# A wait ahead of each input load of batches 2 to 7: four loads under way in a fused attention and token-mixing kernel

## The chip, the cores and the metric

The kernel runs on one core of a Trainium2 chip. The time is in microseconds (us) on the device, from runs of the whole program. Beside it stands one profiled execution, with a trace of every instruction and every DMA packet. Its span runs from the first to the last instruction of the program; the time of the execution contains a little more.

The engines have these names: PE (TensorE, matmuls and transposes; PEld is its loading of weights), DVE (VectorE), ACT (ScalarE), POOL (GpSimd) and SP (SyncE, which only issues DMAs here). L91 is line 91 of the kernel.

## What is computed

Inputs are q, k and v of shape 8 x 8 x 576 x 64 (batch, head, position, head dimension) in float32, and three weight matrices. Attention is done within chunks of 64 positions; its output, seen as 8 x 576 x 512, goes through a layer that mixes positions:

```python
# attention in chunks of 64 positions
scores = scale * np.matmul(q_c, k_c.transpose(0, 1, 2, 4, 3))
scores = scores - np.max(scores, axis=-1, keepdims=True)
attn = np.exp(scores)
attn = attn / (np.sum(attn, axis=-1, keepdims=True) + 1e-09)
out = np.matmul(attn, v_c)
...
# mixing of positions, x of shape 8 x 576 x 512
wq = x @ w_q
wk = x @ w_k
W_tok = scale * np.einsum('bsd,btd->bst', wq, wk)
mixed = np.einsum('bst,btd->bsd', W_tok, x)
return (np.maximum(mixed, 0.0) @ w_out).astype(np.float32)
```

## The kernel before

**Units and batches.** The attention of all 8 batches is cut into 36 units of 8 chunk pairs; a batch is 4.5 units (9 tiles, two to a unit). A unit passes through these stages: `stage_a1` (L365) transposes tiles of q and k on TensorE (L375), `stage_a2` copies them to SBUF on DVE (L385), `stage_b1` makes the scores (L400) and their maxima on DVE (L408), `stage_b2` subtracts them (L414) and takes the exponential on ACT (L422), `stage_c` transposes the result (L429) and copies it (L431), `stage_d1` multiplies with v (L445), `stage_d2` divides by the sums (L457 to L460) and leaves the output in `x_nat`. The loop from L525 overlaps the stages: in step kk it does b1 of unit kk, d1 of unit kk-2, a1 of unit kk+2, c of unit kk-1.

**The mixing layer.** The steps of a batch's mixing layer (`make_moe`, L151) are set into this loop by a plan that is made when the program is built (L472 on). Each engine takes its instructions in the order in which the program lists them; nothing is reordered at run time. The layer's outputs (L320, L338) are copied to `osb` and stored by DMAs on SP's queue (L321, L340).

**The input loads.** All loads are DMAs issued by GpSimd, one after the other; they read float32 and write float16. `load_qk(b, part)` (L85) issues four: q and k, each in two halves of the partitions' heads (`sl`), for tiles 0 to 3 (part 0) or 4 to 8 (part 1). Each writes 128 KB or 160 KB. `load_v(b, part)` (L94) sets the column of ones with a memset (L98) and issues three: one over 128 partitions and two over 64, 128 + 64 + 64 KB or 160 + 80 + 80 KB. A batch has 14 loads. There are two buffers for each kind and part of tile, so the loads of batch b + 2 write where those of batch b were read.

**When they are issued.** The loads of batches 0 and 1 are listed at the start (L119 to L125), v's second part of batch 1 a little later. `reload` (L506) lists a load of batch b + 2 right after the last stage that reads the same part of batch b: `load_qk` after `stage_a1`, `load_v` after `stage_d1`. The weights are loaded behind `load_qk(2, 0)` (four loads, L110 and L111) and behind `load_qk(2, 1)` (two, L115). In the whole program GpSimd issues 118 loads: 64 of q and k, 48 of v, 6 of weights. Apart from memsets and the identity matrix it does nothing else.

**What a load waits for.** The framework gives the loads of GpSimd eight completion semaphores in turn, so a load also waits until the load eight places before it has landed. A load into a used buffer waits for TensorE to have read it.

Of the kernel before, what the change touches and what calls it, by code (L numbers as in the profile page):

```python
# [9 lines left out]
F16 = mybir.dt.float16  # L10
# [7 lines left out]
def kernel(  # L18
# [15 lines left out]
    nc = tc.nc  # L34
    B, H, S, D = q.shape
# [3 lines left out]
    P = 128  # L39
# [12 lines left out]
    const = ctx.enter_context(tc.tile_pool(name="const", bufs=1))  # L52
# [28 lines left out]
    cuts = ((0, 4), (4, NT))  # L81
    v_cuts = ((0, 8), (8, NS))
    data = {}

    def load_qk(b, part):  # L85
        t0, t1 = cuts[part]
        for ti, x in enumerate((q, k)):
            tl = qn_pool.tile([P, 2, t1 - t0, R * D], F16, name=f"qn{ti}{part}", tag=f"qn{ti}{part}")
            of = x[b].rearrange("h s d -> (h s) d").rearrange("(l t p r) d -> l p t (r d)", l=2, p=P, r=R)
            for sl in range(2):  # L90
                nc.gpsimd.dma_start(tl[:, sl], of[sl, :, t0:t1, :])  # L91
            data[b, part, ti] = tl

    def load_v(b, part):  # L94
        n0, n1 = v_cuts[part]
        vt = v_pool.tile([P, 2, n1 - n0, D + 2], F16, name=f"vt{part}", tag=f"vt{part}")
        of = v[b].rearrange("h s d -> (h s) d").rearrange("(l n p) d -> l p n d", l=2, p=P)
        nc.gpsimd.memset(vt[:, :, :, D : D + 1], 1.0)  # L98

        for sl, to, at, rows in ((0, 0, 0, P), (1, 0, CH, CH), (1, CH, 0, CH)):  # L100
            nc.gpsimd.dma_start(vt[to : to + rows, sl, :, 0:D], of[sl, at : at + rows, n0:n1, :])  # L101
        data[b, part, 2] = vt

    def w_rows(w):
# [12 lines left out]


    load_qk(0, 0)  # L119
    load_qk(0, 1)  # L120
    load_v(0, 0)
    load_qk(1, 0)
    load_v(0, 1)
    load_qk(1, 1)
    load_v(1, 0)  # L125

    drain = [False]
# [495 lines left out]
```

## Time and profile before

| | us |
|---|---|
| median of 3 runs | 152.61 (152.55 to 152.71) |
| profiled execution, time | 152.53 |
| its span | 150.7 |
| PE busy | 122.2 (81%) |
| DVE busy | 113.9 (76%) |
| ACT busy | 100.9 (67%) |
| POOL busy | 94.3 (63%) |

The DMA issues by kind (from issue to landing is the median of the group):

| from, to | queue | number, KB each | us from issue to landing |
|---|---|---|---|
| q to `qn` | POOL | 16 of 160, 16 of 128 | 5.5, 6.2 |
| k to `qn` | POOL | 16 of 160, 16 of 128 | 5.9, 5.9 |
| v to `vt` | POOL | 8 of 160, 8 of 128 | 6.9, 7.6 |
| v to `vt` | POOL | 16 of 80, 16 of 64 | 5.9, 6.8 |
| weights to `wout` | POOL | 2 of 256 | 6.6 |
| `osb` to the output | SP | 31 of 256, 9 of 128 | 4.1, 3.0 |
| `wqkT` to `wqd` | SP | 6 of 72 | 5.5 |

How to read the lines that follow below. In the view of slices the span is cut into 40 equal parts of some 3.8 us, and each digit is the busy share of one of them in tenths. In the chain of waits and in the timeline the first number is the start in us from the beginning of the span, the second the duration; `x8` is a run of eight instructions; a bracket holds the idle time of the engine before it and what ended it. The chain follows the work that ended last backwards: at each step to what released it. "issue" in it is time for which the profile shows no cause. A line of the DMA issues names the tile, the queue, the number, the size and the time to landing; asked of a short stretch of time, it tells of a single load. A load's bar on POOL is the time in which GpSimd makes its descriptors; the data move afterwards.

### The profile page before, as it was taken

Reading aid. Unit: us, or ns where it says so; the run is one execution under the profiler, and the core shown is the slowest. Engines: PE = TensorE matmul, PEld = TensorE weight load, DVE = VectorE, ACT = ScalarE, POOL = GpSimd, SP = SyncE. Lnnn points to the kernel's source line nnn. Section 1 sums busy time; section 2 is a strip of 40 time slices with the busy share of each in tenths; the row PEclk is TensorE's granted clock in tenths of the full one; section 3 lists DMA queues with packets and bytes.
Section 4 is the critical chain, followed back from the end, with each engine's and each line's share of the span. In section 5 each row is a group of like instructions: output and inputs, shape, how many; then the busy total and the mean of one; then the engine's idle time right before and its main releaser. Section 6 shows DMA issues by size and latency. Waiting matters only on the chain.

```text
span 150.7 us, 6041 instructions
## 1 busy us (share of the span) xinstructions
PE 122.2 (81%) x2580; PEld 83.0 (55%) x2580; DVE 113.9 (76%) x235; ACT 100.9 (67%) x199; POOL 94.3 (63%) x140
## 2 busy tenths in 40 slices
PE   0267767768686999998979999999879988999970
PEld 0156646556464775684747657766657655554430
DVE  0047997999989889998798899989968897454530
ACT  3004334556658979996888899979986996777130
POOL 8999999999789999968878996986000000000000
PEclk9999995999999999999999999999999999999998
DMA  1999999999999999999999999999922344334484
GB/s 17 147 156 163 163 162 165 113 145 145 168 181 166 167 172 192 199 211 212 255 203 217 173 205 220 229 189 244 214 54 74 73 154 157 112 139 106 177 255 165
DMA packets 83050, 25.08 MB, mean 166 GB/s; under 512 B 77392, under 2 KB 78544, under 8 KB 83024
## 3 DMA queue, kind: packets, MB, share of 16 engines
q0 software_dynamic: 77152, 14.82, 118.1%
q1 hardware_dynamic: 5728, 9.75, 19.1%
q8 instruction: 20, 0.33, 0.9%
q10 hardware_dynamic: 144, 0.13, 0.3%
q14 instruction: 6, 0.05, 0.1%
HBM read 29.62 MB, written 9.44 MB: 259 GB/s over the span
## 4 chain that ended last, share of the span: by engine, by line
PE 40%; DVE 16%; ACT 13%; POOL 12%; DMA 11%; issue 5%; DVEq 0%; ACTq 0%; POOLq 0%
PE op L313 11%; POOL qn L91 8%; DMA qn<-in_k_dram 8%; PE tp L375 5%; DVE x_nat L460 4%; DVE sh L414 4%; PE ep L429 4%; DMA out_dram<-osb 3%; ACT es L422 3%; DVE mx L408 3%; POOL vt L101 3%; ACT osb L141 3%; PE tx L165 3%; DVE qkt L385 3%; PE sp L400 3%
## 5 line engine op out<-in xcount | busy, mean ns | idle before, releaser
L101 POOL DMA_DIRECT2D vt<-in_v_dram x48 | 37.9, 824 | 5.6 <-DMA vt<-in_v_dram 3.1
L431 ACT COPY et<-ep 128x512 f16<-128x512 f16 x36 | 21.4, 595 | 18.5 <-PE ep L429 17.2
L375 PE MATMUL tp<-ident,qn 128*64 128x128 f16 x576 | 26.8, 235 | 8.5 <-DMA qn<-in_q_dram 6.1
L385 DVE COPY qkt<-tp 128x1024 f16<-128x1024 f16 x36 | 24.5, 682 | 9.2 <-PE tp L375 9.1
L313 PE MATMUL op<-wout,rmx 128*128 128x512 f16 x124 | 30.5, 379 | 0.2 <-ACT rmx L147 0.2
L422 ACT ACTIVATE es<-sh 128x512 f16<-128x512 f32 x36 | 23.3, 646 | 10.1 <-DVE sh L414 10.1
L408 DVE TENSOR_REDUCE mx<-sp 128x8 f32<-128x512 f32 x36 | 24.7, 686 | 6.8 <-PE sp L400 6.7
L91 POOL DMA_DIRECT2D qn<-in_k_dram x32 | 26.5, 862 | 3.0 <-PE ep L429 1.1
L375 PEld LDWEIGHTS <-qn 128*64 128x64 f16 x576 | 20.4, 118 | 13.1 <-DMA qn<-in_q_dram 6.5
L414 DVE TENSOR_TENSOR sh<-sp,mx 128x512 f32<-128x512 f32 x36 | 24.9, 692 | 3.5
L91 POOL DMA_DIRECT2D qn<-in_q_dram x32 | 27.1, 881 | 0.5 <-issue 0.4
L460 DVE TENSOR_TENSOR x_nat<-xp,rec 128x512 f16<-128x512 f32 x36 | 24.9, 692 | 1.2
L141 ACT COPY osb<-op 128x512 f32<-128x512 f32 (+1 forms) x29 | 17.1, 598 | 7.1 <-PE op L313 5.6
L400 PEld LDWEIGHTS <-qkt 64*64 64x64 f16 x576 | 12.6, 113 | 15.8 <-issue 5.3
L400 PE MATMUL sp<-qkt 64*64 64x64 f16 x576 | 16.8, 200 | 5.0 <-DVE sh L414 2.1
L445 PE MATMUL xp<-vt,et 64*64 64x65 f16 x576 | 13.2, 198 | 7.3 <-DVE x_nat L460 3.6
L141 ACT COPY xt<-tx 128x768 f16<-128x768 f16 (+1 forms) x23 | 18.2, 792 | 0.9 <-PE tx L165 0.9
L313 PEld LDWEIGHTS <-rmx 128*128 128x128 f16 x124 | 11.2, 98 | 10.2 <-issue 0.6
L147 ACT ACTIVATE rmx<-ma 128x512 f16<-128x512 f32 x28 | 15.4, 610 | 1.1 <-PE ma L251 1.0
L429 PE MATMUL ep<-ident,es 128*128 128x128 f16 x144 | 14.7, 226 | 0.0
L445 PEld LDWEIGHTS <-et 64*64 64x64 f16 x576 | 9.4, 108 | 9.2 <-ACT es L422 5.1
L165 PE MATMUL tx<-ident,x_nat 128*128 128x128 f16 x144 | 12.3, 223 | 0.0
(47 smaller groups left out, 139.9 us busy)
## 6 DMA issues: line engine op xcount, KB each, us to landing
out_dram<-osb SPq DMA_DIRECT2D x31, 256.0 KB, 4.1
qn<-in_q_dram POOLq DMA_DIRECT2D x16, 160.0 KB, 5.5
qn<-in_k_dram POOLq DMA_DIRECT2D x16, 160.0 KB, 5.9
qn<-in_q_dram POOLq DMA_DIRECT2D x16, 128.0 KB, 6.2
qn<-in_k_dram POOLq DMA_DIRECT2D x16, 128.0 KB, 5.9
vt<-in_v_dram POOLq DMA_DIRECT2D x8, 160.0 KB, 6.9
vt<-in_v_dram POOLq DMA_DIRECT2D x16, 80.0 KB, 5.9
out_dram<-osb SPq DMA_DIRECT2D x9, 128.0 KB, 3.0
```

Source lines behind the costliest of these rows:

```text
L91: nc.gpsimd.dma_start(tl[:, sl], of[sl, :, t0:t1, :])
L101: nc.gpsimd.dma_start(vt[to : to + rows, sl, :, 0:D], of[sl, at : at + rows, n0:n1, :])
L141: (nc.vector.tensor_copy if on_vector else nc.scalar.copy)(to, of)
L313: nc.tensor.matmul(op[:], lhsT=rmx[:, i, ds(t * P, P)], rhs=wout16[:, i, :], start=(i == 0), stop=(i == HQ - 1),)
L375: nc.tensor.transpose(tp[CH * sl : CH * sl + CH, j, ti, :, r, :], src[:, sl, r * D : r * D + D], ident[:],)
L385: nc.vector.tensor_copy(qkt[:].rearrange("p j t c k -> p (j t c k)"), tp[:].rearrange("p j t c r g -> p (j t c r g)"),)
L400: nc.tensor.matmul(sp[rows, i ^ sl, :], lhsT=qkt[rows, j, 0, c, :], rhs=qkt[rows, j, 1, c, :], start=True, stop=True,)
L408: nc.vector.tensor_reduce(mx[:], sp[:], axis=AX.X, op=ALU.max)
L414: nc.vector.tensor_tensor(out=sh[:].rearrange("p i (g r) -> p i r g", g=G, r=R), in0=sp[:].rearrange("p i (r g) -> p i r g", g=G, r=R), in ...
L422: nc.scalar.activation(es[:], sh[:], AF.Exp, scale=scale_attn)
L445: nc.tensor.matmul(xv[CH * par : CH * par + CH, sl, m, :], lhsT=et[at : at + CH, m, CH * sl : CH * sl + CH], rhs=vt[at : at + CH, sl, 0 : ...
L460: nc.vector.tensor_tensor(out=x_nat[:, 4 * u : 4 * u + 4, :, :].rearrange("p m l d -> p l m d"), in0=xv[:, :, :, 0:D], in1=rec[:, :, :, No ...
```

## The change

Ahead of each load of batches 2 to 7, GpSimd copies one element of the fourth last load of q, k or v into a scratch tile, `probe`, and then issues the load. The copy reads what that load wrote, so it waits for the landing; GpSimd takes its instructions in order, so the load after it waits too. The list `sent` holds one element of each load of q, k and v, in the order of issue; the loads of weights are not in it and have no copy ahead of them. The loads of batches 0 and 1 enter the list but are not held back.

```diff
+    probe = const.tile([P, 1], F16, name="probe")
+    sent = []
+
+    def send(to, of, paced):
+
+        if paced:
+            last = sent[-4]
+            at = last.start_partition()
+            nc.gpsimd.tensor_copy(probe[at : at + 1], last)
+        nc.gpsimd.dma_start(to, of)
 
     def load_qk(b, part):
...
             for sl in range(2):
-                nc.gpsimd.dma_start(tl[:, sl], of[sl, :, t0:t1, :])
+                send(tl[:, sl], of[sl, :, t0:t1, :], b >= 2)
+                sent.append(tl[0:1, sl, 0, 0:1])
             data[b, part, ti] = tl
 
     def load_v(b, part):
...
         for sl, to, at, rows in ((0, 0, 0, P), (1, 0, CH, CH), (1, CH, 0, CH)):
-            nc.gpsimd.dma_start(vt[to : to + rows, sl, :, 0:D], of[sl, at : at + rows, n0:n1, :])
+            send(vt[to : to + rows, sl, :, 0:D], of[sl, at : at + rows, n0:n1, :], b >= 2)
+            sent.append(vt[to : to + 1, sl, 0, 0:1])
         data[b, part, 2] = vt
```

In the changed kernel the copy is line 92 and the issue line 93.

## The prediction

> **What bounds the kernel now.** I read the engine rows and the slices first, then the chain of waits, then GpSimd's timeline, then the time to landing of single loads.
>
> The chain of waits names GpSimd and the loads only in the first third of the span:
>
> ```profile
> 15.71 2.38 POOL qn L91 x3
> 18.09 5.44 DMA qn<-in_k_dram
> 23.57 0.42 PE tp L375 x2
> ...
> 38.14 0.74 POOL qn L91
> 38.88 0.34 issue
> 39.23 6.26 DMA qn<-in_k_dram
> 45.53 0.30 PE tp L375 x3
> ```
>
> A K load issued at 39.23 lands 6.26 us later, and the transposes L375 start 0.04 after it. Up to here the input sets the pace. Later the chain runs through PE, DVE and ACT, and no input load stands in it. But the loads have not become idle work:
>
> ```profile
> POOL 8999999999789999968878996986000000000000
> DMA  1999999999999999999999999999922344334484
> ```
>
> GpSimd and the DMA engines are busy to slice 28 of 40, about 105 us. So the question for the whole change is how much earlier than needed a load lands. I count the loads of GpSimd from 0 to 117 (64 of q and k, 48 of v, 6 of weights). Load 48 is the one of the chain: it lands at 45.49, when it is wanted. Load 111, the last of k, is issued at 97.83; the issue view of that moment has
>
> ```profile
> qn<-in_k_dram POOLq DMA_DIRECT2D x1, 160.0 KB, 8.3
> ```
>
> so it lands at 106.1. Its first reader is the second quarter of this group of TensorE's timeline, some 0.3 us after its start, at 109.85:
>
> ```profile
> 109.54 0.64 PE L375 MATMUL tp<-ident,qn 128*64 128x128 f16 x16
> ```
>
> The slack there is 3.7 us. Between these two loads the DMA engines supply 63 loads in 60.65 us, 0.963 us each, and the computation wants 63 in 64.3 us, 1.02 us each. The margin is 6%. Anything that makes the mean load cost more than about 1.02 us becomes the kernel's pace.
>
> How many loads are under way? GpSimd already has a limit of eight:
>
> ```profile
> 72.13 0.91 POOL L101 DMA_DIRECT2D vt<-in_v_dram  x1
> 73.72 1.38 POOL L101 DMA_DIRECT2D vt<-in_v_dram  x2 [0.68 <-DMA vt<-in_v_dram]
> ```
>
> The load at 73.72 waits for the load eight before it, issued at 65.51 with 7.92 us to landing, so landed at 73.43: the engine starts 0.29 us after the landing. From load 45 on, six or seven earlier loads are in flight at each issue (starts and landings laid side by side).
>
> **The change, part by part.** It removes nothing and reorders nothing; in the instruction order of the changed kernel GpSimd alone gains 84 copies of one element, one ahead of each load of batches 2 to 7 (14 a batch: 8 of q and k, 6 of v). The weights' six loads and batch 1's last three stay free. Each copy waits for the landing of the fourth last load of q, k or v, and behind it in GpSimd's queue stands everything else of GpSimd: this load, the next memset, every later load. Nothing of SP's queue is behind it. Who waits for those loads is TensorE's L375 and L445.
>
> The first part is the copy's own time. The trace has no such copy. GpSimd's nearest rows are 98 ns for a memset of 128x1 and 287 ns for a select over 128x128; below, the DMA after a v memset starts only 0.05 us after the memset's start (7.91 and 7.96), so it may cost as little as 0.05. I take 0.15, nearer to the memset, keeping 0.05 and 0.29. GpSimd's own work per batch is four issues 0.75 apart, four 0.86 apart and six of v for 4.7, together 11.1 us, plus 0.2 for memsets; fourteen copies at 0.15 make it 13.4, or 0.96 us a load. That alone is still under 1.02. At 0.29 it is 15.4, or 1.10, above it.
>
> The second part is the loop that the wait closes: landing of load n-4, 0.29 us to the start of the copy (if it wakes as the DMA did; 0.04 as TensorE's does is the low end), the copy, then issue to landing with three loads ahead. Four loads pass per turn. Its largest term is the last, and it's not the 5.5 to 7.9 us of the page's medians, which is queueing behind seven. Single issues show what is left with a short queue:
>
> ```profile
> qn<-in_q_dram POOLq DMA_DIRECT2D x1, 128.0 KB, 3.2
> ...
> qn<-in_k_dram POOLq DMA_DIRECT2D x1, 128.0 KB, 4.2
> ...
> qn<-in_q_dram POOLq DMA_DIRECT2D x1, 160.0 KB, 4.3
> ```
>
> These are loads 0, 3 and 4, with none, three and four ahead. Load 4 starts at 4.53 and lands at 8.88; load 0, its fourth last, lands at 4.68, so the cap would issue it at 4.68 + 0.29 + 0.15 = 5.12. Loads land in the order of issue and it would still find a queue, so I leave its landing: 3.76 us. The other row in just the capped state is load 36: issued at 29.28, three ahead, the fourth last landed 0.30 before:
>
> ```profile
> qn<-in_q_dram POOLq DMA_DIRECT2D x1, 160.0 KB, 4.3
> ```
>
> 4.25 us. I take the middle of 3.76 and 4.25, 4.0; the bounds are 3.24 (a lone load) and 4.72 (load 5, four ahead and one of the larger loads). A turn is 4.0 + 0.29 + 0.15 = 4.44 us, 1.11 us a load, above the 1.02 wanted and the 0.96 supplied.
>
> The sum. The first copy stands ahead of load 25 and waits for load 21, which lands at 23.53: load 25 goes out at 23.97 instead of 21.21 and lands at 28.0. In the order that the copies count, load 111 is 80 places later, 20 turns: 88.8 us, 116.8. The free loads use GpSimd too (four of wqk 2.7 us, two of wout 1.3 us), and four turns of four issues leave little room; against it three loads of v go out unpaced. I add 2 us net, with 0 and 4 as bounds. Load 111 then lands at 118.8, 9.0 us after 109.85. The same sum puts load 48 (17 places, 18.9 us, plus 2) at 48.9, 3.4 us late, so the delay begins early and grows. What follows load 111 (40.85 us to the end of the span) keeps its length: the drain has no loads but load 112 to 117, six places or 6.7 us after it, wanted 6.3 and 12.5 us after it, so at most 0.4 us more. Nothing hides the 9 us: TensorE waits in order, and DVE, ACT and the stores are fed by it.
>
> The profiled execution took 152.53 us with a span of 150.7; the median of the runs is 152.61. 152.53 + 9.0 gives 161.5.
>
> One rule of the Trainium skill bears on the loop. The page "DMA: Bandwidth & Descriptors", section "Anatomy of one DMA — SWDGE (gpsimd) path", gives a transfer issued by GpSimd a fixed 2.0 us, mostly the wait for the receipt, plus its bytes over 436 GB/s. For 128 KB that would be an estimated 2.3 us against the 3.2 us of load 0, and a turn of some 2.7 us, under which the cap would cost nothing. The row is the measurement and I go by it; the rule's other side, that a round trip is paid per turn and not per byte, is what a cap of four exposes.
>
> **The rivals.**
> First, the harder cap: the loop is longer than I take, because the stores (256 KB each, from 55 us on) slow the loads in flight, or because the copy costs like the select. For it: after 60 us the DMA engines move 205 to 220 GB/s where they moved 144 at first, and time to landing rises at the same seven ahead from 5.3 to 8.3. Against: most of that rise is queue. With 4.25 + 0.29 + 0.29 = 4.83 a turn, load 111 lands at 28.4 + 96.6 + 2 = 127, 17 us late: 169.7. With 4.72 in place of 4.25 it is 26.5 us, 179.
>
> Second, on the other side: four in flight still keep the DMA engines full, and a shorter queue helps what shares them. The point is a turn of 3.85 us (four times 0.963). It needs issue to landing of 3.4 us at my other terms, just over the lone load's 3.24, or 3.76 with the low ends 0.04 and 0.05. Then the loads keep their pace, the late slack of 3.7 us hides the rest, and the gain would be at the transfers of wqd (72 KB, median 5.5 us), for which TensorE's L251 waits 2.2 us in three places. At most that is won: 150.3; with the delay of the first turns given back against it, 152 to 155. Against it: it needs all low ends together, and GpSimd's 0.96 us a load is beside it.
>
> Third, the cap doesn't bite: this would need the waits to be met already, at the place of issue. They are not: for 92 of the 93 loads from 25 on, the fourth last of all loads lands after the issue (by 1.5 to 5 us from load 45 on). A time of 152.6 would come of it.
>
> **How the numbers follow.** My forecast, 3 to 14 us slower, has 0.62. The harder cap has 0.19, the full engines 0.17 (of it 0.06 faster, 0.02 within 0.2%, 0.09 slower by up to 3 us), no bite 0.02. A difference under 0.2% can't be told from none here. Range: 155 (turn of 4.1 and nothing for the free loads: 28 + 82 = 110, plus the early delay of 2.5 us that stays) to 171 (the harder cap's first sum and a little). Faster 0.06, same 0.04, slower 0.90.
>
> **What would show it.** In the changed profile GpSimd's L92 copies should show the idle time, some 15 to 25 us of it, ended by landings of qn and vt; a copy should take about 0.1 to 0.2 us; time to landing on the page should fall from 5.5 to 7.9 to about 4; GpSimd's row should stay filled to about 115 to 120 us instead of 104; TensorE's L375 should wait for qn in batches 3 to 7, by some 9 us together more than now. DVE and ACT should keep their busy times. I am wrong if the loads land every 0.96 us or faster (the second rival), if the copies take more than 0.3 us, or if TensorE waits and the end does not move, which would mean that the tail had room.

## The result, and the profile after

| | before | changed |
|---|---|---|
| median, us | 152.66 (152.55 to 152.75, 4 runs) | 180.3 (180.23 to 182.66, 4 runs) |
| profiled execution, span, us | 150.7 | 178.5 |
| DVE, ACT busy, us | 113.9, 100.9 | 114.9, 101.9 |
| POOL busy, us | 94.3 | 107.2 |

The ratio of the times is 1.185, with a 95% interval of 1.175 to 1.195: 27.6 us slower. That is outside the range, 155 to 171. Some executions of a kernel take over 1.5% longer than its fastest one; the ratios leave them out, the medians hold them.

First the slices and the shares of the chain of waits of the changed kernel, from its profile page:

```profile
POOL 8999849896288878569658888575874300000000
PEclk9999669969955799996999589999996699999997
DMA  4999999999999999999999999999999914413475
...
DMA 37%; POOL 26%; PE 21%; issue 10%; ACT 2%; DVE 2%; POOLq 0%; ACTq 0%; DVEq 0%
```

GpSimd is occupied to slice 32, 143 us instead of 105, but with holes, and the loads with GpSimd's work for them hold 63% of the chain to the end. The same line of the kernel before:

```profile
PE 40%; DVE 16%; ACT 13%; POOL 12%; DMA 11%; issue 5%; DVEq 0%; ACTq 0%; POOLq 0%
```

There the loads and GpSimd held some 20%, for 3 of the 11% of DMA are stores.

The groups of GpSimd's copies (line, engine, operation, tiles and shape, count, then busy time, mean ns of one, idle time before them and what ended it), and TensorE's list of waits (the tile, what it waited for, us in total, times, the longest), changed and then before:

```profile
L92 POOL COPY probe<-qn 1x1 f16<-1x1 f16 x46 | 8.1, 176 | 12.5 <-DMA qn<-in_k_dram 7.6 <-DMA qn<-in_q_dram 4.2
L92 POOL COPY probe<-vt 1x1 f16<-1x1 f16 x38 | 6.7, 178 | 9.1 <-DMA vt<-in_v_dram 8.5
```

```profile
PE tp L387 <- DMA qn<-in_k_dram: 13.5, 17, 2.3
PE tp L387 <- DMA qn<-in_q_dram: 10.8, 6, 4.6
```

```profile
PE tp L375 <- DMA qn<-in_q_dram: 6.1, 2, 4.7
PE tp L375 <- DMA qn<-in_k_dram: 2.0, 4, 0.8
```

The 84 copies take 0.18 us each and idle 21.6 us in front of them; TensorE waits 24.3 us for q and k where it waited 8.1 before. The time to landing on the profile page fell:

```profile
qn<-in_q_dram POOLq DMA_DIRECT2D x16, 128.0 KB, 3.6
qn<-in_k_dram POOLq DMA_DIRECT2D x16, 128.0 KB, 4.0
qn<-in_q_dram POOLq DMA_DIRECT2D x16, 160.0 KB, 4.7
qn<-in_k_dram POOLq DMA_DIRECT2D x16, 160.0 KB, 4.8
```

from 6.2, 5.9, 5.5 and 5.9. The larger loads stay well above the 4 us that the sum had. So each load is quicker, and the stream of them is slower. The same stretch of 14 us in the view of windows, before and then changed (stretch, its length, busy time and count of PE, PEld, DVE, ACT, POOL, the granted clock, the mean number of DMA packets under way on an engine, GB/s):

```profile
74.00:88.00 14.00, 12.98 (x314) 9.08 (x311) 12.48 (x26) 12.68 (x27) 12.05 (x18) 1.00 1.84 205
```

```profile
74.00:88.00 14.00, 11.62 (x217) 7.68 (x220) 8.11 (x17) 7.36 (x16) 11.79 (x27) 0.88 1.25 152
```

The DMA engines have 1.25 packets under way on average instead of 1.84 and move a quarter less, though the row of the slices calls them busy in both.

Load 25 is issued at 24.78 and lands at 27.84; load 48 lands at 53.52, load 111 at 136.28. TensorE starts on it at once, 26.4 us later than before (109.85). From there to the end of the span it takes 42.2 us, 1.4 more than before; TensorE's granted clock over the last 42 us is 0.91, and a matmul of L325 takes 397 ns in the mean of the whole run where it took 379. Whether the clock is the whole of these 1.4 us wasn't tried.

How a turn of the loop looks, from GpSimd's timeline of the changed kernel:

```profile
68.84 0.18 POOL L92 COPY probe<-qn 1x1 f16<-1x1 f16 x1
69.03 0.71 POOL L93 DMA_DIRECT2D vt<-in_v_dram  x1
...
73.28 0.18 POOL L92 COPY probe<-vt 1x1 f16<-1x1 f16 x1 [2.21 <-DMA vt<-in_v_dram]
73.73 0.86 POOL L93 DMA_DIRECT2D qn<-in_q_dram  x1 [0.27 <-issue]
74.59 0.18 POOL L92 COPY probe<-vt 1x1 f16<-1x1 f16 x1
74.71 0.84 POOL L93 DMA_DIRECT2D qn<-in_k_dram  x1
```

Load 63 landed at 73.16. The copy that waited for it starts 0.12 later, takes 0.18, and the DMA behind it starts another 0.27 later: 0.57 us from landing to issue. A copy that finds its load landed mostly delays the DMA behind it by 0.12 only (74.59 to 74.71). The three loads after load 63 landed at 74.13, 74.60 and 76.12, in part closer together than the 0.98 us that GpSimd takes here from one issue to the next (73.73 to 74.71). So landings come in bunches and issues don't.

I take the mean of two terms over the held loads 25 to 111: from the landing of the fourth last to the issue ("gap"), and from the issue to its own landing. Predicted were 0.44 and 4.0, a turn of 4.44; measured are 0.93 and 4.43, a turn of 5.36. Twenty turns at 0.92 more are 18.4 us. With 161.5 less the 2 us for the weights (they are within the measured turns) and 1.4 for the tail that makes 179.3, of the 180.24 us of the profiled execution. This mean runs over two stretches that differ: the one up to load 48, in which GpSimd also issues the six loads of weights, and the one behind it. The experiments take them apart.

### The profile page after: what moved, and what is told of

Read it like the earlier page. It is cut to its first block, busy times and chain, and to the rows that moved or that the text cites. A ratio compares the mean times of both kernels' runs of the same rounds, so it can differ in the third digit from the quotient of the medians.

```text
span 178.5 us, 6162 instructions
## 1 busy us (share of the span) xinstructions
PE 137.1 (77%) x2580; PEld 90.8 (51%) x2580; DVE 114.9 (64%) x235; ACT 101.9 (57%) x199; POOL 107.2 (60%) x224
## 4 chain that ended last, share of the span: by engine, by line
DMA 37%; POOL 26%; PE 21%; issue 10%; ACT 2%; DVE 2%; POOLq 0%; ACTq 0%; DVEq 0%
DMA vt<-in_v_dram 17%; DMA qn<-in_k_dram 15%; POOL qn L93 15%; PE op L325 9%; DMA qn<-in_q_dram 6%; POOL vt L93 4%; POOL probe L92 4%; PE tp L387 2%; PE opt L342 2%; PE tx L177 1%; PE ep L441 1%; PE gp L248 1%; PE sp L412 1%; ACT osb L153 1%; PE wpa L195 1%
## 5 line engine op out<-in xcount | busy, mean ns | idle before, releaser
L387 PE MATMUL tp<-ident,qn 128*64 128x128 f16 x576 | 33.1, 248 | 24.6 <-DMA qn<-in_k_dram 13.5
L387 PEld LDWEIGHTS <-qn 128*64 128x64 f16 x576 | 23.2, 124 | 32.7 <-DMA qn<-in_k_dram 17.0
L397 DVE COPY qkt<-tp 128x1024 f16<-128x1024 f16 x36 | 24.5, 682 | 22.0 <-PE tp L387 21.7
L420 DVE TENSOR_REDUCE mx<-sp 128x8 f32<-128x512 f32 x36 | 24.7, 686 | 20.2 <-PE sp L412 19.9
L325 PE MATMUL op<-wout,rmx 128*128 128x512 f16 x124 | 32.5, 397 | 0.2 <-ACT rmx L159 0.2
L93 POOL DMA_DIRECT2D qn<-in_q_dram x32 | 26.4, 836 | 5.9 <-DMA vt<-in_v_dram 2.0
L93 POOL DMA_DIRECT2D qn<-in_k_dram x32 | 25.9, 823 | 0.2
L412 PEld LDWEIGHTS <-qkt 64*64 64x64 f16 x576 | 13.2, 118 | 14.9 <-issue 5.8
L457 PE MATMUL xp<-vt,et 64*64 64x65 f16 x576 | 14.2, 203 | 8.1 <-DVE x_nat L472 2.8
L325 PEld LDWEIGHTS <-rmx 128*128 128x128 f16 x124 | 11.7, 102 | 11.3 <-issue 2.5
L441 PE MATMUL ep<-ident,es 128*128 128x128 f16 x144 | 16.2, 243 | 0.0
L92 POOL COPY probe<-qn 1x1 f16<-1x1 f16 x46 | 8.1, 176 | 12.5 <-DMA qn<-in_k_dram 7.6
L457 PEld LDWEIGHTS <-et 64*64 64x64 f16 x576 | 10.1, 112 | 10.1 <-ACT es L434 4.1
```

Source lines behind the costliest of these rows:

```text
L93: nc.gpsimd.dma_start(to, of)
L325: nc.tensor.matmul(op[:], lhsT=rmx[:, i, ds(t * P, P)], rhs=wout16[:, i, :], start=(i == 0), stop=(i == HQ - 1),)
L387: nc.tensor.transpose(tp[CH * sl : CH * sl + CH, j, ti, :, r, :], src[:, sl, r * D : r * D + D], ident[:],)
L397: nc.vector.tensor_copy(qkt[:].rearrange("p j t c k -> p (j t c k)"), tp[:].rearrange("p j t c r g -> p (j t c r g)"),)
L412: nc.tensor.matmul(sp[rows, i ^ sl, :], lhsT=qkt[rows, j, 0, c, :], rhs=qkt[rows, j, 1, c, :], start=True, stop=True,)
L420: nc.vector.tensor_reduce(mx[:], sp[:], axis=AX.X, op=ALU.max)
```

## The experiments

The questions were: is it the wait or the copies; does the turn have a fixed length; and what makes a turn of 5.36 us out of the expected 4.44.

**Copies alone, and five and six under way.** The edits, each by itself:

```diff
-            last = sent[-4]
+            last = sent[-9]   # e1; in e2 sent[-5], in e3 sent[-6]
```

> All 84 copies stay, but each reads an element of the ninth last load, which has landed already, so no wait is added. Theory (the wait for the fourth last landing is what costs): a copy in front of a load adds some 0.12 us to GpSimd's pace, 0.93 us a load, still under the 1.02 us that the computation wants, so 152 to 155 us, loads still landing with 6 to 7 in flight. Rival (GpSimd's own time: a copy of 0.18 us plus 0.27 us until the DMA behind it starts, 84 times): 1.2 us or more a load, 165 to 178 us.

Measured: 152.52 us, ratio 0.995 (0.988 to 1.002). The copies by themselves cost nothing; the rival, GpSimd's own time, falls.

> The copy reads the fifth last load. Theory (a turn of a nearly fixed length that lets N loads pass): the turn stays at about 5.4 us plus a little queue, so 1.1 us a load, load 111 lands near 116 to 120 and the time is 158 to 166 us. Rival (each wait costs the same, whatever the number under way): 175 to 180 us. Rival (the DMA engines' bandwidth is the bound): the same as with four, 180.

> The copy reads the sixth last load. Theory: 5.6 us a turn over six loads is 0.93 us a load, under the 1.02 that is wanted: 152.5 to 156 us. Rival (each wait costs the same): over 170 us.

Measured: 170.23 us with five (ratio 1.112, 1.105 to 1.120) and 161.16 with six (1.051, 1.044 to 1.059). Both are above what the theory gave: the turn isn't fixed. From the traces it is 5.36, 6.14 and 6.80 us with four, five and six under way, and per place of the loads that are counted 1.36, 1.26 and 1.16 us (load 25 to load 111 over 80 places). The three turns lie near 2.5 us plus 0.7 us a load, as if each load more added its own service to the turn and the 2.5 us beside it were spread over more loads. From load 48 on a place takes 1.31, 1.22 and 1.12 us, where it took 0.96 before the change. Six are still above the 1.02 us that is wanted.

**The last batch alone.**

```diff
-                send(tl[:, sl], of[sl, :, t0:t1, :], b >= 2)
+                send(tl[:, sl], of[sl, :, t0:t1, :], b >= 7)
```

and the same for v.

> Only the 14 loads of the last batch are held to four. Theory (a load's lateness counts only beyond its slack): loads 101 to 117 land 4 to 12 us ahead of their readers before; fourteen places at 0.35 us more are 5 us, so load 111 is 0 to 3 us late and the time 152.5 to 156 us. Rival (every held load costs a third of a microsecond of the whole, 27.7 us over 84 loads): 157.2 us.

Measured: 153.37 us, ratio 1.002 (0.995 to 1.009). Fourteen held loads vanish in the slack, as the theory has it; the loss isn't a price per wait but a pace kept up for longer than the slack lasts.

**Without the stores.** The output stores of batches 0 to 6 are left out, in the changed kernel and in the one before:

```diff
-                nc.sync.dma_start(out[b, ds(t * P, P), :], osb[:])
+                if b == B - 1:
+                    nc.sync.dma_start(out[b, ds(t * P, P), :], osb[:])
```

and likewise for the tails (L340).

> The changed kernel without the output stores of batches 0 to 6 (those of batch 7 stay). Theory (bursts of 256 KB stores make the loads under way late, 4.4 us instead of the 3.8 us of the stretch without stores): issue to landing falls to 3.8 us, the turn from 5.4 to some 4.7, 14 us over 20 turns less: 164 to 170 us. Rival (the stores don't matter to the loop): 178 to 181 us.

> The kernel before without the output stores of batches 0 to 6: the measure for the run beside it. Theory: before, the loads ran ahead of the computation from batch 4 on, so the stores cost next to nothing: 150 to 153 us. Rival (stores slow the loads there as well and set the pace): under 148 us.

Measured: 171.48 us (ratio to the kernel before 1.117, 1.107 to 1.127) and 149.82 (0.976, 0.967 to 0.985). Both miss what the theories gave, 164 to 170 and, just, 150 to 153. The capped kernel gains 8.8 us by the medians, some 10 by the ratios, which compare within one session; the kernel before gains some 4 (0.976). Without the stores the cap costs 21.7 us, with them 27.6, so they add about 6 us to the loss: part of the cause, not most of it. Issue to landing falls from 4.43 to 4.06, not to 3.8.

**The weights first.** The six loads of weights, which have no copy ahead of them, are listed before the first held load:

```diff
     load_v(1, 0)
+    load_wqk()
+    load_wout()
```

> The changed kernel with the six loads of weights listed ahead of the first held load. Theory (the two 256 KB loads of w_out, which are not counted, stand in front of loads 42 to 48 and make one turn some 5 us longer): issue to landing of loads 42 to 48 falls from 6 to about 4 us and the time by 2 to 6 us, 174 to 178 us. Rival (moved work only shifts the delay to the start): 179 to 182 us.

Measured: 178.43 us, its runs between 175.04 and 180.74, too far apart for a verdict. The trace (of the execution of 180.74 us) shows the local part: loads 42 to 48 take 3.6 us to land in the mean instead of 5.3, and between the landings of the first held load and of load 48, 17 places, 19.9 us pass instead of 25.7. But the six loads now go ahead of these places. Load 48 lands at 50.96 instead of 53.52, and load 111 at 136.48, no earlier than the 136.28 of the changed kernel. What of it would reach the time stays open.

**The loads alone.** To measure the loop by itself, all loads and copies stay in their order and the whole computation is left out but for one copy and one store at the end.

> All 118 loads and 84 copies of the changed kernel in their order, and nothing else: the whole computation is left out, but for one copy and one store at the end. Theory (the loop is long by itself: some 2.5 us of round trip in each turn that the other loads don't fill, plus 0.6 to 0.7 us a load): a turn of 4.9 to 5.3 us, 1.22 to 1.32 us a place. Rival (the loop alone is as short as predicted, 4.4 us, and it is the stores and the waits for buffers that stretch it): 1.05 to 1.12 us a place.

> The same with the second last load in place of the fourth last. Theory (turn = 2.5 us + 0.65 us for each load under way): 3.8 to 4.0 us a turn, 1.9 to 2.0 us a place. Rival (a turn of fixed length): 4.9 to 5.3 us, 2.5 us a place.

> The same with copies that read the ninth last load, which has landed. Theory: without a wait the pace is that of GpSimd with its copies or of the DMA engines, 0.85 to 0.97 us a place, whatever is under way. Rival (the copies themselves set the pace of the capped run): as with four, 1.1 us or more.

Measured, with one run of each, from load 25 to load 111: 1.20 us a place with four under way (a turn of 4.71: gap 0.96, issue to landing 3.75), 1.87 with two (3.77: 0.58 and 3.19), 0.99 without a wait. The turn isn't fixed, 3.77 with two against 4.71 with four.

These means hold the stretch of the weights. Behind it, from load 48 on, a place takes 1.11 us with four under way (gap 0.90, issue to landing 3.60), 1.83 with two and 0.92 without a wait. So the loop alone is there as short as predicted: 63 places take 70.2 us, and the prediction had 1.11 us for each, 69.9. The rival is right on this point and the theory's 1.22 to 1.32 is not; the pace without a wait lies in the expected 0.85 to 0.97.

With two under way the round trip lies bare; GpSimd's row and the DMA engines' in the slices of that run:

```profile
POOL 8999538548256465464645554455455554656451
DMA  4999949978957997989779769797796968889975
```

GpSimd is at work for 58% of the time, waits for the rest, and even the DMA engines have holes. With two, the gap is mostly the bare 0.57. With four it is longer, because by the time a landing comes GpSimd often still works on the issue before it: so it was for 56 of the 63 loads behind load 48, with a gap of 0.94 us in the mean, against 0.57 for the other seven.

**What the computation adds.** The two stretches side by side, in us from landing to landing:

| | load 25 to 48, 17 places | load 48 to 111, 63 places |
|---|---|---|
| the prediction's sum | 20.9 | 69.9 |
| loads alone, four under way | 25.7 | 70.2 |
| changed kernel without stores | 25.7 | 76.3 |
| changed kernel | 25.7 | 82.8 |
| kernel before | 19.4 | 60.7 |

Up to load 48 the computation adds nothing to the loads alone. Behind it the computation without stores adds 6.1 us and the stores another 6.5. In the run without stores the times to landing run like those of the loads alone for many loads and differ for a few in a row. Those were the loads in flight while a DMA packet of 16 KB of the queue that the profile calls "instruction" was under way. Two more runs of the loads alone, with work on TensorE that waits for no load (`busy` is a tile in PSUM, `ones` a tile of ones in SBUF):

```diff
+    for n in range(2560):          # e11
+        nc.tensor.transpose(busy[:, n % 8, :], ident[:], ident[:])
...
+    for n in range(640):           # e12
+        nc.tensor.matmul(busy[:], lhsT=ident[:], rhs=ones[:], start=True, stop=True)
```

> The loads alone, four under way, and beside them 2560 transposes of the identity matrix on TensorE that wait for no load: 5120 instructions, as many as in the whole kernel; the computation is left out. Theory (a packet of 16 KB that fetches instructions holds one of the 16 DMA engines for about 1 us, and a load lands only when its slowest engine has finished): some 20 such packets, 3 to 6 us more over the 80 places, 1.23 to 1.28 us a place against 1.20 of the loads alone, and the late loads are those under way at a packet. Rival (no such effect; something else in the computation makes the loads later): 1.19 to 1.21.

> The same with 640 matmuls of 512 columns instead, about as long on TensorE but 1280 instructions. Theory: a quarter of the packets, so 0.5 to 1.5 us over the 80 places, 1.20 to 1.22 us a place. Rival (a busy TensorE makes the loads later, by its reads of SBUF, whatever its instructions): the same as with many instructions.

Measured, with one run of each and from load 25 to load 111: 1.316 and 1.238 us a place, against 1.198. TensorE is busy for 98% of both spans, so the difference between the two isn't its being busy; what differs is the number of instructions and with it the line of the instruction queue, in the run with many and then with few:

```profile
q8 instruction: 20, 0.33, 0.9%
```

```profile
q8 instruction: 5, 0.08, 0.2%
```

Both cost more than expected, 9.4 and 3.2 us over the 80 places, with 15 and 3 such packets between the landings of loads 25 and 111: 0.6 and 1.1 us for each. The second is a single difference of 3 us, so a share of some 1 us that a busy TensorE adds by itself isn't excluded.

The times to landing show the packets' part load by load. I compare each load from 49 to 111 with the same load in the loads alone, and count it as hit if a 16 KB packet was under way between 1.6 us after its issue (when the first packets of load 0 start, before the change) and its landing. In the run with many instructions the 34 loads that were hit landed 0.81 us later than alone, the other 29 landed 0.07 later. In the changed kernel without stores it is 0.59 for 31 and 0.03 for 32, and with the stores 1.18 for 30 and 0.43 for 33. One such packet, seen in the DMA view of the run with many instructions from 79.9 to 81.6 us, in 40 slices of 0.04 us:

```profile
DMA  9999999999999999999997543221000000000002
GB/s 123 120 491 85 88 72 90 81 114 108 133 136 136 121 142 127 106 78 61 60 66 48 33 30 21 18 18 9 0 0 0 0 0 0 0 0 0 0 3 15
...
q8 instruction: 1, 0.02, 5.7%
```

The jump to 491 GB/s is the 16 KB packet. It lasts 1.56 us by the trace, to 81.58. The other engines run dry one after the other, and for some 0.4 us toward the end this packet alone is under way; packets of the loads start again as it ends. The trace doesn't name a packet's engine; I read this as the parts of the loads that go through the one engine standing behind the packet. GpSimd can't send new work meanwhile, for its copy waits for just these loads (the one issued at 77.61 lands at 82.88):

```profile
81.21 0.74 POOL L93 DMA_DIRECT2D qn<-in_q_dram  x1
83.01 0.18 POOL L92 COPY probe<-vt 1x1 f16<-1x1 f16 x1 [1.05 <-DMA vt<-in_v_dram]
```

The kernel before fetches the same 20 packets (21 us of packet time on single engines), with six or seven loads in flight. That the other engines have work queued there meanwhile, so that it costs less, is my reading and wasn't tried.

The Trainium skill tells of this fetch in "Runtime: NRT & Kernel Launch", section "Instruction fetch mechanics": blocks of 16 KiB or 256 instructions, by a DMA queue of the sequencer's own, the cost mostly hidden. The count agrees (5160 instructions of TensorE, 20 packets). Hidden it is for TensorE, which is busy for 98% of the span in the run with many instructions, but not for the loads under way beside it.

## Why the prediction was wrong

Right in kind, wrong in size: the direction and the mechanism (a loop from landing to issue that passes four loads a turn) were as forecast. The rival nearest by its number is the first, the harder cap, at the upper of the two sums that it had (179). That is partly luck: its reason, stores that slow the loads in flight, is one of several that came, and its turn of 4.72 + 0.29 + 0.29 = 5.30 us was put together of other parts than the measured 4.43 and 0.93.

- **What bounds the kernel, and the margin of 6%** held. The copies alone change nothing, the last batch alone changes nothing, and above 1.02 us a load the loads set the pace (six under way: 8 us slower).
- **The copy's time**, 0.15 us, is 0.18 and fits.
- **The start**, load 25 at 28.0, is 27.84, by two errors that cancel: it was issued at 24.78, not 23.97, and landed 3.06 us later, not 4.0.
- **The step that failed most is the issue to landing in "A turn is 4.0 + 0.29 + 0.15 = 4.44 us".** It was read off loads 4 and 36, issued at 4.53 and 29.28, before the first store (55.4), and the sum had no term for what the kernel does beside the loads. Behind load 48 the loads alone take 3.60 us to land, the kernel without stores 3.91, the changed kernel 4.38. So 63 places took 82.8 us instead of 69.9, 12.9 us more. The stores are 6.5 of it. The other 6.1 came with the computation, and there the lateness sits on the loads under way at a fetch of instructions (0.59 us for 31 of them, 0.03 for the rest). No run took the fetches out of the kernel itself.
- **The 0.44 from landing to issue** was wrong too, but it costs nothing on balance. It is 0.57 where the wait binds, since the start of the DMA behind a copy that waited was left out (0.27), and 0.90 in the loads alone behind load 48, since GpSimd is often still busy with the issue before. I had held GpSimd's pace of 0.96 us a load against the wanted 1.02 as a bound of its own, but it stands in the loop. But the loads alone land after 3.60 us there, not 4.0. They come to the predicted turn because the two errors cancel: 0.90 + 3.60 = 4.50.
- **The 2 us for the free loads** was the second step that failed. The sum had 18.9 + 2 us up to load 48, which was to land at 48.9; it took 25.7, and load 48 landed at 53.52. That is 4.8 us, as much in the loads alone, so it isn't the computation. In these 25.7 us GpSimd issues 23 loads, the six of weights among them, so 1.12 us for each: a load of weights cost as much as any other. With the weights first the same 17 places took 19.9.
- **The tail**, said to keep its length, grew by 1.4 us.
- Together: 12.9 and 4.8 and 1.4, less 0.2 at the start, make 18.9 of the 18.7 us between 161.5 and the profiled 180.24.
- **Of the signs**, the idle time ahead of the copies (21.6 us) and the copy's time came as said; GpSimd's row runs to 143 us and not 115 to 120, and TensorE waits 16 us more for q and k and not 9.
- **The second rival**, four in flight keep the engines full, is excluded by the loads alone: 1.11 us a place behind load 48 against 0.92 without a wait, with no store and no computation beside them. **The third**, no bite, by 21.6 us of idle time ahead of the copies.

I had also set bounds on issue to landing (3.24 to 4.72) that hold the measured mean. The upper end of the range, 171, didn't use them: it rested on the harder cap's first sum, with 4.25. With 4.72 the same sum gives 179.

## What to carry to other kernels

A limit on loads under way costs nothing only if the loads that stay under way outlast the round trip from a landing through the waiting engine to new data, with every hiccup of a DMA engine in it. Here the turn was some 2.5 us beside about 0.7 us for each load, with four to six under way. By an estimate from these turns eight would make 1.01 us a load, barely enough for a need of 1.02; the kernel before, with its limit of eight, ran at 0.96 behind load 48. Six under way cost 8 us, and each one fewer from there 9 to 10.

Take the terms of such a loop under the traffic that will run beside it. The turn put together from quiet rows held for the loads alone; the kernel took 18% longer (82.8 us instead of 69.9 for 63 places). And count every load that goes through the issuing engine: six that had no wait of their own cost as much as those that had one.

## What I had not expected

- A fetch of instructions delays input loads: one packet of 16 KB, about 1 us long, made the loads under way 0.6 to 0.8 us later than the same loads alone, and cost the capped loop 0.6 us where it was seen 15 times. Whether a deeper queue hides it wasn't tried.
- A copy on GpSimd that waited for a DMA holds the next DMA 0.57 us from the landing; one that didn't wait mostly holds it 0.12 us.
- The DMA row of the slices is no measure of the flow: it is 9 in the stretch of 14 us above both at 205 GB/s and at 152.
